# Two v loads of an attention-and-MLP kernel moved on SyncE's queue

## The chip, the cores and the metric

The kernel runs on one core of one Trainium2 chip. The metric is the device time in microseconds (us) of that core, as the median of the runs; smaller is better. Engines are named as in the profile: PE (TensorE, matmul), PEld (its weight loads), DVE (VectorE), ACT (ScalarE), POOL (GpSimd), SP (SyncE, which here only issues DMAs).

## What is computed

Attention over 8 batch rows, 8 heads, 576 positions, head size 64, followed by a two-layer MLP with a squared ReLU. Half of the heads see a sliding window of 32 positions, the other half a dilated one: every fourth position back to 128.

```python
scores = scale * np.matmul(q, k.transpose(0, 1, 3, 2))
mask_plain = (rel >= 0) & (rel < window)                                        # 32
mask_dil = (rel >= 0) & (rel < window * dilation) & (rel % dilation == 0)      # dilation 4
attn = softmax(where(mask, scores, -1e9));  x = attn @ v                        # by head
h = x @ w_in;  out = (np.maximum(h, 0) ** 2) @ w_out                            # 4608 tokens, 512 -> 2048 -> 512
```

## The kernel before

**Rows and stages.** A "row" is one of the 8 batch entries (576 tokens). The MLP works on 9 chunks of 512 tokens. The loop at the end of the kernel (L1039) has one stage for each chunk c from 1 to 8; in stage c the MLP matmuls of chunk c run, and between them, at hand-written steps (`PLANS`, L1023), the parts of the attention of row b = c + 1, and the scores of row b + 1 near the end of the stage. The parts are named by letters (`row_parts`): s0 and s1 are the scores of the sliding heads (PE L638), z0 and z1 those of the dilated ones (PE L653), each followed by the exponential on ACT (L619) and the mask on DVE (L623); a0 to a2 are the products with v of the sliding heads (PE L693), d0, d1, e0, e1 those of the dilated ones (PE L720), each followed by the division on DVE (L676, L677); x and y are transposes of the results on PE (L742, L757), copied by ACT.

**The MLP.** First layer: matmuls at L291, ReLU on ACT (L300), square into `g` on DVE (L325). From stage 2 on the second layer multiplies in seven products of sums (L443), and DVE forms the sums S1 to S3 from `g` (L423 to L429).

**How q, k and v of a row come in.** All tiles here exist once or twice, in turns by the row's parity.

- q and k, sliding heads: POOL asks for `n` (L156); DVE or ACT brings it into token order, `o` (L259 on ACT; for row 4 all of it there; L261 on DVE); SP stores `o` to DRAM, `dp` (`keep_sliding_qk`, L267), and two transposing loads bring it back, `QKTp` (`transpose_sliding`, L275, k first, then q).
- q and k, dilated heads: POOL copies them within DRAM, `dd` (`keep_dilated_qk`, L249); two transposing loads bring them in, `QKTd` (`transpose_dilated`, L279).
- v, dilated heads: two loads of 288 KB into `sd` (`load_dilated_v`, L176 and L180), cast on POOL into `vd` (L235, L237).
- v, sliding heads: six loads of 96 KB into `sv` (`load_sliding_v`, L168), cast on POOL into `vp` (L218, L222). `load_v(b, True)` asks for the dilated loads and then the sliding ones.

**What sets the order.** The schedule is manual: each engine and each queue does its instructions in the order in which the program writes them. All loads of v, the stores, and all transposing loads are on SP's queue; an SP instruction that waits holds all that stand behind it. POOL first does a tiny copy (`see`, L204) that waits for the k half of the last `QKTp`, then asks for `n` and `dd` of the next row, then casts v of the present row.

At the start of stage c (row b = c + 1) the program writes: POOL's look, the loads of `n` and `dd` of row b + 1; from row 4 on SP's `transpose_dilated(b + 1)`; for b = 3 SP's `load_sliding_v(3)`. At step `ORDER[c]` of the stage (46, 33, 9, 2, 2 for c = 1 to 5) it writes `turn_and_load` for row b + 1: the copy into token order, the store, the transposing loads, and the loads of v. Row 3 is turned in stage 1, row 4 in stage 2 (88 to 123 us in the profile), row 5 in stage 3. `CROSS` is 5.

Of the kernel before, what the change touches and what calls it, by code (L numbers as in the profile page):

```python
# [17 lines left out]
def kernel(  # L18
# [134 lines left out]
    def load_whole_sliding_qk(b):  # L153
        n = natp.tile([P, HH, 9, D], FP16, name=f"n{b}", tag="n")
        for i, s in ((1, k), (0, q)):
            nc.gpsimd.dma_start(  # L156
                out=n[64 * i : 64 * (i + 1)],
                in_=s[b, 0:HH].rearrange("h (p j) d -> p h j d", j=9),
            )
        return n  # L160
# [4 lines left out]
    def load_sliding_v(b, m0=0, m1=NB):  # L165
        for m in range(m0, m1):
            lo = QB * m - PADP
            nc.sync.dma_start(  # L168
                out=sv[PADP:P, m, :, :],
                in_=v[b, 0:HH, lo + PADP : lo + P, :].transpose([1, 0, 2]),  # L170
            )

    def load_dilated_v(b, t):
        vv = v[b, HH:H].rearrange("h (i c) d -> i h (c d)", c=DIL)
        if t == 0:
            nc.sync.dma_start(out=sd[PADD:P, 0, :, :], in_=vv[0:QD])  # L176
            return
        if b == 0:
            nc.sync.dma_start(out=sd[0:PADE, 1, :, :], in_=vv[QD - PADE : QD])
        nc.sync.dma_start(out=sd[PADE : PADE + QD, 1, :, :], in_=vv[QD:CL])  # L180

    def load_v(b, dilated_first=False):
        if not dilated_first:
            load_sliding_v(b)
        for t in range(2):
            load_dilated_v(b, t)
        if dilated_first:
            load_sliding_v(b)
# [13 lines left out]
    def see(landed):  # L202

        nc.gpsimd.tensor_copy(look, landed)  # L204
# [34 lines left out]
    def cast_v(b):  # L239
        sliding = [lambda mp=mp: cast_sliding_v(b, mp) for mp in range(NB // 2)]  # L240
        dilated = [lambda t=t, a=a: cast_dilated_v(b, t, a) for t in (0, 1) for a in range(2)]
        return dilated + sliding
# [3 lines left out]
    def keep_dilated_qk(b):  # L246
        d = dpool.tile([2, HH * CL, DIL * D], FP16, name=f"dd{b}", tag="dd")
        for i, src in ((1, k), (0, q)):
            nc.gpsimd.dma_start(  # L249
                out=d[i], in_=src[b, HH:H].rearrange("h (i c) d -> (h i) (c d)", c=DIL)  # L250
            )
        return d

    def in_token_order(b, n):
        o = natp.tile([P, 9, HH, D], FP16, name=f"o{b}", tag="o")
        i = n.rearrange("p h j d -> p j h d")
        j = {2: 6, 3: 6, 4: 9}.get(b, 0)
        if j > 0:
            nc.scalar.copy(o[:, 0:j], i[:, 0:j])  # L259
        if j < 9:  # L260
            nc.vector.tensor_copy(o[:, j:9], i[:, j:9])  # L261
        return o

    def keep_sliding_qk(b, o):
        d = dpool.tile([2, S, HH * D], FP16, name=f"dp{b}", tag="dp")
        for i in (1, 0):
            nc.sync.dma_start(  # L267
                out=d[i].rearrange("(p j) x -> p (j x)", j=9),
                in_=o[64 * i : 64 * (i + 1)].rearrange("p j h d -> p (j h d)"),
            )  # L270
        return d

    def transpose_sliding(b, dp):
        for i in (1, 0):
            nc.sync.dma_start_transpose(out=QKTp[b % 2][:, i, :, PADP:], in_=dp[i])  # L275

    def transpose_dilated(b, dd):
        for i in (1, 0):
            nc.sync.dma_start_transpose(out=QKTd[b % 2][:, i, :, KPAD : KPAD + S], in_=dd[i])  # L279
# [117 lines left out]
    def sum_w_out_gen():  # L397

        for name, pool, tag, w in (("T1", n1p, "nd", 36), ("T2", n1p, "nd", 36), ("T3", n1p, "ns", 36)):
            u = pool.tile([P, w * D], FP16, name=name, tag=tag, bufs=2 if tag == "nd" else 1)  # L400
            T[name] = u[:, 0 : HF * HT].rearrange("p (j t) -> p j t", j=HF)
        for j in range(2):
            f = slice(4 * j, 4 * j + 4)
            b11, b12 = wo[j][:, :, 0:HT], wo[j][:, :, HT:DM]
            b21, b22 = wo[2 + j][:, :, 0:HT], wo[2 + j][:, :, HT:DM]
            for o, a, b in (
                ("T1", b12, b11),
                ("T3", b22, b12),
                ("T2", b22, T["T1"][:, f, :]),
                ("T4", b21, T["T2"][:, f, :]),  # L410
            ):
                nc.vector.tensor_sub(T[o][:, f, :], a, b)
                yield
# [127 lines left out]
    def moe_gen(c):  # L541
        yield from mm1_gen(c)
        yield from mm2_gen(c)

    def moe_seven_gen(c):
        turns["bank"] = 0
        yield from mm1_gen(c, lambda f2: sums_behind(c, f2))
        yield from seven_gen(c)
# [15 lines left out]
    CROSS = 5  # L564
# [231 lines left out]
    def run(*plans, more=()):  # L796


        todo = list(more)
        for plan, parts in plans:  # L800
            for w in plan.split():
                step, *names = w.split(":")
                todo += [(int(step), parts[n]) for n in names]
        at = 0
        for step, part in sorted(todo, key=lambda t: t[0]):
            pump(step - at)
            at = max(at, step)
            part()
        pump(1000)
# [174 lines left out]
    n, dd = load_whole_sliding_qk(2), keep_dilated_qk(2)  # L984
# [2 lines left out]
        for a in range(2):  # L987
            cast_dilated_v(1, t, a)

    def turn(b, n, dd):  # L990
        dp = keep_sliding_qk(b, in_token_order(b, n))
        if b < 4:
            transpose_dilated(b, dd)
        transpose_sliding(b, dp)

    pending.append(mm2_by_rows_gen(0))
    parts = row_parts(1, True)
# [9 lines left out]
            " 25:d1 26:e0 28:e1 29:y0 30:y1",  # L1007
            parts,
        ),
        more=[(25, lambda: turn(2, n, dd))],  # L1010
    )
    load_v(2, True)
    kept[0]()
# [25 lines left out]
    for c in range(1, NTOKC):  # L1039
        b = c + 1  # L1040
        more = []
        casts = cast_v(b) if b < B else []
        if c == 1:

            for cast in casts[:2]:
                cast()
            casts = casts[2:]
            see(sv[PADP : PADP + 1, 3, 0, 0:1])
            more.append((41, kept[1]))
        if b + 1 < B:  # L1050
            see(QKTp[b % 2][0:1, 1, 0, PADP : PADP + 1])
            if b > CROSS:

                see(xT[(b - 1) % RING][0:1, 1, S - 1 : S])
            n, dd = load_whole_sliding_qk(b + 1), keep_dilated_qk(b + 1)

            def turn_and_load(b=b + 1, n=n, dd=dd):
                turn(b, n, dd)
                load_dilated_v(b, 0)
                load_dilated_v(b, 1)  # L1060
                if b > 3 and b <= CROSS:
                    load_sliding_v(b)

            if b + 1 > 3:
                transpose_dilated(b + 1, dd)
            if b == 3:
                load_sliding_v(3)
            more.append((ORDER[c], turn_and_load))
            if b >= CROSS:
                more.append((38, lambda b=b + 1: load_sliding_v(b)))  # L1070
        for cast in casts:
            cast()
        if c == 1:
            it = sum_w_out_gen()
            more += [(2 + 3 * i, lambda it=it: next(it)) for i in range(8)]
        pending.append(moe_gen(c) if c < SEVEN else moe_seven_gen(c))
        now, ahead = PLANS.get(c, ("", ""))
        run((now, rows_.get(b)), (ahead, rows_.get(b + 1)), more=more)
# [30 lines left out]
```

## Time and profile before

| | |
|---|---|
| median of 3 runs | 300.04 us (299.71 to 300.9) |
| the profiled execution's own time | 301.48 us |
| its span, first to last instruction | 299.7 us |
| mean granted TensorE clock | 0.999 |
| PE busy | 287.7 us, 96% of the span |
| DVE, ACT, POOL busy | 202.3, 176.2, 96.6 us |
| DMA moved | 45.59 MB, 152 GB/s over the span |

The profile is one execution, seen instruction by instruction. "Busy" is time in which an engine worked, not in which it was needed: an engine that is idle and is waited for by nobody costs nothing. A line of a timeline gives start, length, engine, line of the kernel, operation, and out<-in tiles; "idle before" and what released the engine follow in brackets. The windows view gives, for each stretch of time, the length, the busy time of PE, PEld, DVE, ACT and POOL with the number of instructions in brackets, the granted clock, the busy share of the DMA engines, and GB/s. The chain of waits is followed back from the last instruction, at each step to what released it.

### The profile page before, as it was taken

To read this page: it belongs to the slowest core of one execution; us is meant where nothing else is said; L and a number is where in the kernel's file an instruction comes from. 1 tells how busy PE (TensorE), PEld (TensorE's weight loads), DVE (VectorE), ACT (ScalarE), POOL (GpSimd) and SP (SyncE) were. 2 spreads that over 40 slices of the span, in tenths; PEclk is the share of its full clock that TensorE was granted. 3 is DMA by queue.
4 is the path that set the end of the run, shared out by engine and by line. 5 is a ranking of instruction groups with operands and counts; after the bars stand their busy time and mean duration, and the time that the engine had idled before them with its cause. 6 is when DMAs were issued, how large, how long until landed. Compare 5 with 4: busy or idle time off the path is not lost.

```text
span 299.7 us, 7125 instructions
## 1 busy us (share of the span) xinstructions
PE 287.7 (96%) x2880; PEld 202.7 (68%) x2880; DVE 202.3 (67%) x371; ACT 176.2 (59%) x331; POOL 96.6 (32%) x153
## 2 busy tenths in 40 slices
PE   2899999999999998999999999999999999999995
PEld 2678945565554577656889988558765875785584
DVE  7686646778633997499688867896878624733662
ACT  1668854778548773766646657664766267425611
POOL 8492009403914604752563019308400000000000
PEclk9999999999999999999999999999999999999999
DMA  7999999799999888998999799989124130003013
GB/s 129 205 159 214 210 212 159 154 174 263 196 195 241 179 154 148 215 270 176 186 229 251 144 169 186 255 187 166 72 92 24 39 131 11 0 2 141 3 35 105
DMA packets 73969, 45.59 MB, mean 152 GB/s; under 512 B 56720, under 2 KB 67600, under 8 KB 73744
## 3 DMA queue, kind: packets, MB, share of 16 engines
q1 hardware_dynamic: 66544, 31.37, 49.0%
q0 software_dynamic: 7248, 13.63, 25.7%
q8 instruction: 22, 0.36, 0.5%
q10 hardware_dynamic: 144, 0.13, 0.1%
q14 instruction: 11, 0.09, 0.1%
HBM read 36.83 MB, written 16.52 MB: 178 GB/s over the span
## 4 chain that ended last, share of the span: by engine, by line
PE 72%; DMA 11%; POOL 6%; DVE 5%; issue 2%; SPq 1%; ACT 1%; POOLq 0%; DVEq 0%; ACTq 0%
PE PS L291 34%; PE PS L443 25%; PE PS L332 6%; DMA nd<-in_k_dram 5%; DMA sv<-in_v_dram 3%; DMA sd<-in_v_dram 3%; PE PS L720 2%; PE PS L693 2%; PE PS L653 1%; POOL vp L222 1%; DVE AT L623 1%; POOL vp L218 1%; ACT AT L619 1%; DVE S L429 1%; PE PS L638 1%
## 5 line engine op out<-in xcount | busy, mean ns | idle before, releaser
L291 PE MATMUL PS<-xr,wi 128*128 128x512 f16 (+3 forms) x704 | 133.5, 341 | 0.3 <-ACT xr L749 0.2
L300 ACT ACTIVATE rt<-PS 128x512 f16<-128x512 f32 (+2 forms) x160 | 88.4, 557 | 42.9 <-PE PS L291 40.0
L291 PEld LDWEIGHTS <-wi 128*128 128x128 f16 x704 | 75.8, 113 | 38.5 <-issue 0.5
L325 DVE TENSOR_TENSOR g<-rt 128x1024 f16<-128x1024 f16 (+1 forms) x64 | 45.7, 714 | 28.6 <-ACT rt L300 28.3
L619 ACT ACTIVATE AT<-PS 128x576 f16<-128x576 f32 x64 | 38.4, 652 | 15.5 <-PE PS L653 8.0
L443 PEld LDWEIGHTS <-S 128*128 128x128 f16 x448 | 42.8, 98 | 6.0 <-issue 0.6
L443 PE MATMUL PS<-T,S 128*128 128x256 f16 x336 | 39.6, 273 | 0.0
L443 PEld LDWEIGHTS <-g 128*128 128x128 f16 x336 | 32.2, 98 | 5.6 <-DVE g L325 0.4
L235 POOL CAST vd<-sd 128x512 f16<-128x512 f32 x32 | 23.6, 762 | 36.8 <-DMA sd<-in_v_dram 36.0
L332 PE MATMUL PS<-wo,g 128*128 128x512 f16 x128 | 33.1, 379 | 0.0
L443 PE MATMUL PS<-wo,g 128*128 128x256 f16 x224 | 26.6, 273 | 0.1
L218 POOL CAST vp<-sv 128x512 f16<-128x512 f32 x24 | 17.2, 716 | 23.3 <-DMA sv<-in_v_dram 16.3
L677 DVE TENSOR_TENSOR y<-PS,rcp 72x512 f16<-72x512 f32 (+1 forms) x32 | 22.0, 687 | 1.1
L623 DVE TENSOR_TENSOR AT<-AT,maskd 128x1152 f16<-128x1152 f16 x14 | 11.5, 818 | 15.2 <-ACT AT L619 15.1
L623 DVE TENSOR_TENSOR AT<-AT,maskp 128x1152 f16<-128x1152 f16 x14 | 14.5, 1036 | 10.3 <-ACT AT L619 10.3
L677 DVE TENSOR_TENSOR x<-PS,rcp 96x512 f16<-96x512 f32 (+1 forms) x25 | 16.6, 665 | 0.9
L222 POOL CAST vp<-sv 32x512 f16<-32x512 f32 (+1 forms) x24 | 16.7, 697 | 1.5
L720 PEld LDWEIGHTS <-AT 128*128 128x128 f16 x256 | 11.9, 100 | 6.8 <-DVE y L677 2.0
L332 PEld LDWEIGHTS <-g 128*128 128x128 f16 x128 | 10.3, 98 | 8.0
L429 DVE TENSOR_TENSOR S<-g,S 128x1024 f16<-128x1024 f16 x14 | 10.7, 804 | 7.4 <-PE PS L443 7.4
L676 DVE RECIPROCAL rcp<-PS 96x8 f32<-96x8 f32 (+3 forms) x57 | 11.2, 197 | 4.9 <-PE PS L720 2.9
L443 PE MATMUL PS<-T,g 128*128 128x256 f16 x112 | 14.2, 273 | 0.0
(93 smaller groups left out, 283.2 us busy)
## 6 DMA issues: line engine op xcount, KB each, us to landing
out_dram<-c SPq DMA_DIRECT2D x12, 512.0 KB
sv<-in_v_dram SPq DMA_DIRECT2D x48, 96.0 KB, 4.9
sd<-in_v_dram SPq DMA_DIRECT2D x16, 288.0 KB
dp<-o SPq DMA_DIRECT2D x12, 288.0 KB
wo<-in_moe_w_out_dram POOLq DMA_DIRECT2D x4, 512.0 KB, 14.3
n<-in_k_dram POOLq DMA_DIRECT2D x6, 288.0 KB, 6.0
n<-in_q_dram POOLq DMA_DIRECT2D x6, 288.0 KB, 6.8
dd<-in_k_dram POOLq DMA_DIRECT2D x6, 288.0 KB, 8.1
```

The lines of the kernel that those rows point to most:

```text
L218: nc.gpsimd.tensor_copy(vp[b % 2][:, m : m + 2, :, 0:D], sv[:, m : m + 2, :, :])
L222: nc.gpsimd.tensor_copy(vp[b % 2][0:PADP, m:m1, :, 0:D], sv[P - PADP : P, m - 1 : m1 - 1])
L235: nc.gpsimd.tensor_copy(o, by_class(sd[:, t]))
L291: nc.tensor.matmul(ph[:, o : o + b - a], w_in_of(dmk, ffc), xr[:, dmk, a:b], start=(dmk == 0 and o == 0), stop=(dmk == NDM - 1 and o + b - ...
L300: nc.scalar.activation(rt, ph[:, 0:w], ACTF.Relu)
L325: nc.vector.tensor_mul(g[:, f2 : f2 + 2, o:TOKC], rt[:, :, o:TOKC], rt[:, :, o:TOKC])
L332: nc.tensor.matmul(po, g[:, ffc, o + t * P : o + (t + 1) * P], w_out_of(ffc), start=(ffc == 0), stop=(ffc == NFF - 1),)
L443: nc.tensor.matmul(po[t], lhs(j)[:, t * P : (t + 1) * P], rhs(j), start=j == 0 and not on_top, stop=j == HF - 1, skip_group_check=on_top,)
L619: nc.scalar.activation(AT[:, u + i, 0:UW], ps[:, :, 0 : UW // 2], ACTF.Exp, scale=scale)
L623: nc.vector.tensor_mul(AT[:, u : u + n, 0:UW], AT[:, u : u + n, 0:UW], mask,)
L677: nc.vector.tensor_tensor(out=x, in0=pv[:, :, :, 0:D], in1=rcp[0:w, 0:i, 0:j].unsqueeze(3).to_broadcast([w, i, j, D]), op=ALU.mult,)
L720: nc.tensor.matmul(pav[:, e, h * (D + 2) : h * (D + 2) + D + 1], AT[:, 4 + 2 * a + t, off : off + P], vd[b % 2][:, t, 2 * a + e, h, 0 : D ...
```

## The change

Three lines are touched in what the program does.

- Stage 2, start: `load_sliding_v(3)`, six issues on SP, stands ahead of `transpose_dilated(4)`, two issues on SP, and no longer behind it.
- Row 4's turn in stage 2: the loads of its v, first the dilated ones and then the sliding ones (eight issues on SP), stand between the store of `o` (`keep_sliding_qk(4)`) and `transpose_sliding(4)`. Before, they stood behind `transpose_sliding(4)`.
- `turn` is written out in `turn_and_load` and keeps its old form for row 2 alone. For rows 2, 3, 5, 6 and 7 the order is as before.

```diff
-    def turn(b, n, dd):
-        dp = keep_sliding_qk(b, in_token_order(b, n))
-        if b < 4:
-            transpose_dilated(b, dd)
-        transpose_sliding(b, dp)
+    def turn(n, dd):
+        dp = keep_sliding_qk(2, in_token_order(2, n))
+        transpose_dilated(2, dd)
+        transpose_sliding(2, dp)
...
             def turn_and_load(b=b + 1, n=n, dd=dd):
-                turn(b, n, dd)
-                load_dilated_v(b, 0)
-                load_dilated_v(b, 1)
-                if b > 3 and b <= CROSS:
+                dp = keep_sliding_qk(b, in_token_order(b, n))
+                if b == 3:
+                    transpose_dilated(b, dd)
+                if b == 4:
+
+                    load_v(b, True)
+                transpose_sliding(b, dp)
+                if b != 4:
+                    load_dilated_v(b, 0)
+                    load_dilated_v(b, 1)
+                if b == CROSS:
                     load_sliding_v(b)
 
+            if b == 3:
+                load_sliding_v(3)
             if b + 1 > 3:
                 transpose_dilated(b + 1, dd)
-            if b == 3:
-                load_sliding_v(3)
             more.append((ORDER[c], turn_and_load))
```

More of the change, by code (lines that the diff above doesn't have):

```diff
@@ L1009 @@
         ),
-        more=[(25, lambda: turn(2, n, dd))],
+        more=[(25, lambda: turn(n, dd))],
     )
```

## The prediction

> **What bounds the kernel now.** I read the page first, then the windows of 2 us around the stretch that the change touches, then the chain of work in order of time, then the timelines of SP, POOL, DVE and PE from 88 to 146 us. TensorE is busy nearly all the time:
>
> ```profile
> PE 287.7 (96%) x2880; PEld 202.7 (68%) x2880; DVE 202.3 (67%) x371; ACT 176.2 (59%) x331; POOL 96.6 (32%) x153
> ```
>
> The other engines end below 70%. So only idle time of PE can be won, and the 12.0 us of it lie mostly at the two ends (6.2 in the first 20 us, 3.5 in the last 20). In the touched stretch the windows give (us, then PE busy, PEld, DVE, ACT, POOL):
>
> ```profile
> 108.00:110.00 2.00, 1.88 (x20) 1.45 (x19) 1.93 (x5) 2.00 (x4) 0.00 (x0) 1.00 1.04 143
> ...
> 112.00:114.00 2.00, 1.48 (x19) 1.13 (x17) 1.97 (x4) 0.00 (x0) 1.87 (x3) 1.00 0.84 182
> ...
> 118.00:120.00 2.00, 1.69 (x21) 1.39 (x18) 1.93 (x6) 0.68 (x3) 0.00 (x0) 1.00 1.22 86
> ...
> 132.00:134.00 2.00, 1.64 (x15) 0.81 (x13) 1.93 (x6) 1.13 (x3) 0.49 (x1) 1.00 1.44 366
> ```
>
> PE lacks 0.12, 0.52, 0.31 and 0.36 us in these four and 0.16 at 134 to 136: 1.47 us in all, 0.5% of the time. That is the whole purse of this change in its own stretch. The 0.52 is the one that it aims at; the chain (start, us, what) shows it:
>
> ```profile
> 106.00 1.29 SPq L279
> 107.39 1.28 SPq L168
> 108.77 0.43 SPq L168
> 109.25 0.46 SPq L168
> 109.82 2.65 DMA sv<-in_v_dram
> 112.54 0.71 POOL vp L222
> 113.29 0.29 PE PS L693 x4
> ```
>
> Row 4's dilated transposes (L279) hold SP until 107.3, only then row 3's sliding v (L168) is asked for, POOL casts it, and PE's first product with it (L693, part a0) starts 0.51 us late. The waits of the windows put those 0.5 us down to POOL vp L222. SP's own order, start and length:
>
> ```profile
> 104.59 2.70 SPq L279 DMA_TRANSPOSE QKTd<-dd  x2
> 107.39 3.89 SPq L168 DMA_DIRECT2D sv<-in_v_dram  x6
> 111.82 1.15 SPq L267 DMA_DIRECT2D dp<-o  x2
> 115.11 2.87 SPq L275 DMA_TRANSPOSE QKTp<-dp  x2
> 118.07 1.36 SPq L176 DMA_DIRECT2D sd<-in_v_dram  x1
> 119.49 0.40 SPq L180 DMA_DIRECT2D sd<-in_v_dram  x1
> 119.99 4.11 SPq L168 DMA_DIRECT2D sv<-in_v_dram  x6
> ```
>
> SP is free at 96.07 (the last store, L362, 95.48 + 0.59) and then stands still for 8.5 us: the waits of SP put it down to dd, which lands at 104.5.
>
> **The change, part by part.** Both edits only move DMA issues on SP; nothing is added or taken away on any engine.
>
> Edit 1: six loads sv (96 KB each) go ahead of two transposes. They come to stand at 96.07, take 3.9 us of SP as now, and are all issued by 100.0, inside the 8.5 us in which SP stood still. Their buffer is free: POOL's casts of row 2 end at 83.3. Landing takes 2.5 us (median now, quiet) to 6.0 us (median of the loads at 120, beside other transfers), so by 102.5 to 106.0. POOL is idle from 102.57 to 111.83 and casts at once.
>
> (a) PE's wait for a0 goes: **-0.51 us**. The next wait, 0.31 at 119.24 (PE L742 for DVE x L677), hangs on part z0's exp and mask, which PE itself starts at 114.82; it moves along and stays.
>
> (b) The six casts take 4.5 us (111.83 to 116.29). They now run at about 104 to 108.5, where DVE is busy 3.86 of 4.00 us, instead of after 111.8. What a cast does to DVE, the lines of g (L325, ns min/median/max) show, first with POOL casting (96.7 to 102.1), then with POOL idle (103.5 to 111.5):
>
> ```profile
> L325 DVE TENSOR_TENSOR g<-rt x3: 1095/1095/1098, 97.3 to 102.0; 128x1024 f16<-128x1024 f16 x3
> L325 DVE TENSOR_TENSOR g<-rt x3: 676/676/678, 103.9 to 108.9; 128x1024 f16<-128x1024 f16 x3
> ```
>
> So +0.42 us for each such operation. Against these very casts the row is milder: two S subtractions (L423) took 1.91 us at 111.88, where 0.68 each is their median: +0.27 each; and g at 159.09 and 188.97 lost nothing beside casts (POOL did). Between 104 and 108.5 stand three: g at 106.15, S at 106.75 and 107.46. Three at 0 to 0.42 is 0 to 1.26; I take three at 0.27, the row of the same casts: **+0.8 us**. It lies on the path: DVE has no gap from 97.3 to 111.0, and PE's weight load waited 0.40 us for g (L325) at 109.64. What DVE wins back at 111.88 (0.54) hides: DVE idles 1.77 us at 116.39 for ACT.
>
> The SBUF — State Buffer page of the Trainium skill ("Who interferes with whom") says that a DVE instruction with two SBUF inputs and a GpSimd one that reads SBUF exclude each other, the second being blocked to the end of the first. The trace agrees in kind: L677, with one input in PSUM, keeps 0.69 us all along. By that rule an operation could wait out a whole cast (0.61), three of them 1.8, and the time would be an estimated 301.3.
>
> (c) Row 4's dilated transposes wait for dd anyway. The added 576 KB share the DMA engines with dd; at the 250 to 280 GB/s of 96 to 102 us that is 0 to 2.3 us, so the pair starts between 104.6 and 106.9 (first one). Its reader, z0 at PE (L653, 114.82), needs it landed, a median of 4.3 us after an issue. The second is issued 1.4 after the first: 108.3 + 4.3 = 112.6 at the latest. Cost **0**, hidden by 2.2 us; if that cover went, PE would wait for the excess.
>
> Edit 2: row 4's eight v loads go between the store of o (dp, L267) and its transposes (L275). Queued behind them on SP: the two transposes, and behind these the stores of the third stage (L483) and row 5's dilated transposes, which wait for dd of row 5 at 130 to 133 in any case. With edit 1, dp no longer waits for SP but for ACT's copy of o (107.39 + 2.10 = 109.49): it goes at 109.6, not 111.82, ended by 110.8. The eight loads take 5.4 us in row 5's turn (143.11 to 148.51), 6.0 in row 4's. So L275 starts at 116.2 to 116.8, not 115.11: **1.1 to 1.7 us later**. Its first transposed half (k) landed just before POOL's look at 120.19, 5.1 us after the issue. 5.1 after 116.2 is 121.3. But 1152 KB of v are now in flight ahead of it on the same queue: at 180 GB/s (112 to 116 us) 6.4 us from about 112.5, to 118.9, where the first transposing packets of before ran 1.1 us after the issue: 1.5 us more. k lands at 121.3 to 122.8, q about 1 us later: 122.3 to 123.8. PE reads it at 124.25 (s0, L638), or 123.7 if (a) came in full. Cost **0**, by a margin of 0 to 2 us. This is the thinnest cover of the change.
>
> POOL's look also holds row 5's loads of n and dd, and row 4's casts. It comes 1.1 to 2.6 us later; n of row 5 then has no v beside it: 5.1 us (row 3, 74 us) or 6.2 (row 7) for its second half instead of 7.8. Issued at 123.1 to 124.0, it lands by 128.2 to 130.2, DVE's copy (L261) stands at 130.78. The casts vd start at 124.3 to 125.8 instead of 123.21 without their waits for sd (0.19 and 0.63); the first is read at 127.71. Cost 0. The casts vp, which now wait until 133.51 with v in hand late, follow at once; they are first read at 136.01, so that gains nothing.
>
> Sum: -0.51 + 0.8 = **+0.3 us**. The profiled execution took 301.48 (span 299.7 and 1.8 around it), 1.4 above the median of the runs; 301.48 becomes 301.8, and the median 300.04 becomes **300.3**.
>
> **The rivals.**
> 1. The casts do no harm. For: at 157 to 160 and 187 to 190 POOL gave way, not DVE. Against: L325's 1.095 in every case from 97 to 102. Then only (a) is left: 300.04 - 0.51 = **299.5**.
> 2. Slower: row 4's sliding transposes land too late for s0. The point is 123.7: if q lands later, PE waits for the excess, and the chain of exp, mask and y behind it (DVE without a gap from 126.1 to 134) shifts by as much, so that nothing is given back. Price: L483 sat 4.5 us on SP at 124.2, right behind the same eight loads; if the transposes are held like that, even half of it (2.25) puts q at 124.5 to 126, up to 2.3 us late: 300.3 + 2 = **302.3**. The DMA: Bandwidth & Descriptors page of the Trainium skill ("Queues, rings and completion order") says that on each DMA engine the descriptors of one ring are consumed in ring order. By that the transposes wait for all of v, which is the 1.5 us above; the trace of before, where nothing of SP's was ahead of them but dp, cannot show it.
> 3. The change does not do what it says: the sv loads are asked for at 96 but land after the stores and beside n and dd, which are still at work at 102, or SP holds them as it held L361 (3.2 us at 92.24); v comes only little before 111, and both terms shrink: **300.0**.
>
> **How the numbers follow.** The forecast (casts cost 0.3 to 1.3, transposes in time) has 0.50, its own range 299.8 to 300.8; rival 1 has 0.20 (299.2 to 299.8); rival 2 has 0.22 (301.0 to 303.5); rival 3 has 0.08. A measurement of this kernel can tell about 0.5% from no change, that is 1.5 us: 298.5 and 301.5. Faster by that needs all 1.47 us of the purse: 0.03. Slower: most of rival 2 (0.18) and the tail of (b) with a late n (0.05): 0.23. The rest, 0.74, is the same. The range 299.4 to 302.2 leaves out half of rival 1 and some two fifths of rival 2.
>
> **What would show it.** In the changed kernel's trace: sv at SP by 96 to 100, and no wait of PE for POOL vp L222 near 113 (edit 1 right); L325 and the S operations between 103 and 111 at 0.9 to 1.1 us instead of 0.68, and PE lacking more than 0.12 us at 108 to 112 (term b right; at 0.68 rival 1 holds); L275 at 116 to 117 and POOL's look at 121 to 123; PE with no gap ahead of L638 near 124 (if there is one, rival 2). The forecast is wrong if sv lands only after 110, or if PE idles over 0.3 us ahead of s0.

## The result and the profile after

| | before | changed |
|---|---|---|
| median of 17 runs | 300.04 us (299.23 to 301.02) | 303.48 us (300.37 to 305.03) |
| ratio, 95% interval | | 1.0080 (1.0059 to 1.0102) |
| the profiled execution, its span | 301.48, 299.7 | 302.32, 300.5 |

The change makes the kernel 0.8% slower, some 2.4 us; the time lies above the predicted range. The ratio is formed from undisturbed runs and is not the quotient of the medians of all runs, which lie 3.4 us apart. The changed kernel's runs fall in two groups by the mean granted clock beside each: nine at 1.000 with a median of 302.1 us, eight at 0.994 with 303.9. The profiled execution is of the first group, near its median. The two spans differ by only 0.8 us because the profiled execution of the kernel before was 1.4 us above that kernel's median.

SP after the change (start, length, line, operation):

```profile
94.62 10.33 SPq L168 DMA_DIRECT2D sv<-in_v_dram  x6
105.11 4.67 SPq L279 DMA_TRANSPOSE QKTd<-dd  x2
110.31 1.14 SPq L267 DMA_DIRECT2D dp<-o  x2
111.55 0.87 SPq L176 DMA_DIRECT2D sd<-in_v_dram  x1
112.47 1.16 SPq L180 DMA_DIRECT2D sd<-in_v_dram  x1
113.73 4.43 SPq L168 DMA_DIRECT2D sv<-in_v_dram  x6
118.27 3.99 SPq L275 DMA_TRANSPOSE QKTp<-dp  x2
122.36 1.73 SPq L483 DMA_DIRECT2D out_dram<-c  x2
```

Row 3's sv is asked for 12.8 us earlier, row 4's transposes (L275) 3.2 us later, and the two stores of stage 2 (L483), which went at 124.20 and took 6.11 us of SP, now go at 122.36 in 1.73. In the kernel before:

```profile
124.20 6.11 SPq L483 DMA_DIRECT2D out_dram<-c  x2
```

There both came behind the requests for row 5's n (120.73 and 121.37): the first held SP for 4.5 us, and the second was issued only at 128.8. Now the first is issued ahead of these requests (123.69 and 124.33), and the second at 123.7, with the first of them. That last move is the one to keep in mind.

The windows of the changed kernel (us, then PE, PEld, DVE, ACT, POOL busy, clock, DMA share, GB/s):

```profile
108.00:110.00 2.00, 1.59 (x16) 1.19 (x14) 1.93 (x5) 2.00 (x4) 1.94 (x2) 1.00 0.52 108
...
112.00:114.00 2.00, 2.00 (x26) 1.82 (x24) 2.00 (x4) 0.45 (x1) 1.33 (x2) 1.00 0.96 237
...
124.00:126.00 2.00, 1.59 (x18) 0.87 (x17) 0.03 (x1) 1.76 (x4) 2.00 (x5) 1.00 1.03 347
...
130.00:132.00 2.00, 1.36 (x13) 0.58 (x12) 1.97 (x4) 1.20 (x2) 1.87 (x3) 1.00 1.39 282
132.00:134.00 2.00, 1.63 (x18) 0.84 (x15) 1.97 (x4) 0.60 (x1) 1.81 (x4) 1.00 0.28 55
```

The 0.52 us at 112 to 114 are won, as wanted; 0.29 more are lost at 108 to 110 (DVE beside POOL's casts). New losses stand at 122 to 126 (0.60: PE's L638 waits for QKTp) and at 130 to 134 (1.01 instead of 0.36). From 120 to 140 us PE is busy 18.25 us instead of 19.48. Of the 1.01 us, 0.64 is a wait for y (L677) that the kernel before does not have, and 0.37 one that it has too (0.36). Where the first comes from, DVE shows, first before, then changed; the last lines are POOL's casts and PE's wait in the changed kernel:

```profile
126.13 0.78 DVE L623 TENSOR_TENSOR AT<-AT,maskp 128x1152 f16<-128x1152 f16 x1 [1.95 <-ACT AT L619]
```

```profile
125.97 1.79 DVE L623 TENSOR_TENSOR AT<-AT,maskp 128x1152 f16<-128x1152 f16 x1 [2.30 <-ACT AT L619]
131.03 0.69 DVE L677 TENSOR_TENSOR y<-PS,rcp 72x512 f16<-72x512 f32 x1
131.64 1.34 DVE L261 COPY o<-n 128x2304 f16<-128x2304 f16 x1
125.94 2.30 POOL L235 CAST vd<-sd 128x512 f16<-128x512 f32 x3
131.77 0.43 PE L720 MATMUL PS<-vd,AT 128*128 128x65 f16 x8 [0.64 <-DVE y L677]
```

The mask (L623) starts as POOL's casts of row 4's vd start, which the late look has moved there, and takes 1.0 us longer. DVE has no gap from there on, so y is late by it.

Row 5's n is no cause of loss in this execution, but it was just in time:

```profile
124.33 6.82 DMA n<-in_q_dram
131.15 0.04 DVEq L261
131.19 0.45 issue
131.64 1.34 DVE o L261
```

DVE's copy of row 5's q and k into token order (L261) needs n and stands between two divisions (y, L677) for which PE waits. It follows the y ahead of it by 0.61 us, as in the kernel before (0.60); an n that lands later than 131.15 would hold it, and the y behind it.

### The profile page after: what moved, and what is told of

It reads as the page before. It is cut to its first block, busy times and chain, and to the rows that moved or that the text cites. A ratio compares the mean times of both kernels' runs of the same rounds, so it can differ in the third digit from the quotient of the medians.

```text
span 300.5 us, 7125 instructions
## 1 busy us (share of the span) xinstructions
PE 287.6 (96%) x2880; PEld 202.1 (67%) x2880; DVE 203.6 (68%) x371; ACT 176.5 (59%) x331; POOL 97.6 (32%) x153
## 4 chain that ended last, share of the span: by engine, by line
PE 64%; DMA 16%; POOL 8%; issue 6%; DVE 4%; ACT 1%; SPq 1%; POOLq 0%; DVEq 0%
PE PS L291 30%; PE PS L443 22%; PE PS L332 6%; DMA sv<-in_v_dram 6%; DMA nd<-in_k_dram 5%; DMA sd<-in_v_dram 3%; DMA n<-in_q_dram 2%; POOL vp L218 2%; PE PS L720 2%; POOL vp L222 2%; PE PS L693 1%; DVE S L429 1%; PE PS L653 1%; ACT AT L619 1%; DVE AT L623 1%
## 5 line engine op out<-in xcount | busy, mean ns | idle before, releaser
L325 DVE TENSOR_TENSOR g<-rt 128x1024 f16<-128x1024 f16 (+1 forms) x64 | 46.7, 730 | 28.1 <-ACT rt L300 27.8
L235 POOL CAST vd<-sd 128x512 f16<-128x512 f32 x32 | 24.6, 794 | 39.0 <-DMA sd<-in_v_dram 38.4
L677 DVE TENSOR_TENSOR y<-PS,rcp 72x512 f16<-72x512 f32 (+1 forms) x32 | 22.0, 686 | 1.1
L623 DVE TENSOR_TENSOR AT<-AT,maskp 128x1152 f16<-128x1152 f16 x14 | 14.3, 1022 | 10.7 <-ACT AT L619 10.7
L623 DVE TENSOR_TENSOR AT<-AT,maskd 128x1152 f16<-128x1152 f16 x14 | 11.6, 829 | 14.3 <-ACT AT L619 14.2
L677 DVE TENSOR_TENSOR x<-PS,rcp 96x512 f16<-96x512 f32 (+1 forms) x25 | 16.6, 665 | 0.9
L222 POOL CAST vp<-sv 32x512 f16<-32x512 f32 (+1 forms) x24 | 15.9, 663 | 1.5
L332 PEld LDWEIGHTS <-g 128*128 128x128 f16 x128 | 10.3, 97 | 8.0
L720 PE MATMUL PS<-vd,AT 128*128 128x65 f16 x256 | 13.7, 197 | 0.8 <-DVE y L677 0.8
```

The lines of the kernel that those rows point to most:

```text
L222: nc.gpsimd.tensor_copy(vp[b % 2][0:PADP, m:m1, :, 0:D], sv[P - PADP : P, m - 1 : m1 - 1])
L235: nc.gpsimd.tensor_copy(o, by_class(sd[:, t]))
L325: nc.vector.tensor_mul(g[:, f2 : f2 + 2, o:TOKC], rt[:, :, o:TOKC], rt[:, :, o:TOKC])
L332: nc.tensor.matmul(po, g[:, ffc, o + t * P : o + (t + 1) * P], w_out_of(ffc), start=(ffc == 0), stop=(ffc == NFF - 1),)
L623: nc.vector.tensor_mul(AT[:, u : u + n, 0:UW], AT[:, u : u + n, 0:UW], mask,)
L677: nc.vector.tensor_tensor(out=x, in0=pv[:, :, :, 0:D], in1=rcp[0:w, 0:i, 0:j].unsqueeze(3).to_broadcast([w, i, j, D]), op=ALU.mult,)
```

## The experiments

Theories: **A**, the loss is the second edit's (A1: row 5's n late, so DVE's copy, y and PE late, and at a long gap the clock; A2: PE's wait for QKTp; A3: POOL's casts beside DVE's masks; later A4: why n is late). **B**, it is the first edit's: the moved casts. **C**, TensorE's clock drops after PE's gaps. Ratios are to the kernel before on the same chip, with 95% intervals.

**The changed kernel again** (`both`, no edit).

> The changed kernel unaltered, for comparison with the parts on one chip. All theories: 301 to 304 us, +2.4 us over before (0.8%). Its times fall in two groups by the mean granted clock that stands beside each: 1.000 (median 302.1 of nine runs so far) and 0.994 (median 303.9 of eight). Theory C (TensorE's clock is halved for a stretch after its gaps near 124 to 134 us) expects runs with 0.994 here too, and, if the profiled one is among them, a stretch of half clock within 10 us behind those gaps.

302.34 us, 1.0063 (1.0034 to 1.0093); 4 of 12 runs at a clock of about 0.994 or below. The profiled one (301.49, look at 122.46) was not among them. In it neither PE waits for QKTp nor DVE for n; the mask takes 1.59 us, and PE waits 0.72 for the y behind it.

**The first edit alone** (`first_only`).

```diff
-                if b == 4:
-                    load_v(b, True)
                 transpose_sliding(b, dp)
+                if b == 4:
+                    load_v(b, True)
```

> Row 3's sv ahead of row 4's dilated transposes; row 4's v stays behind its sliding transposes. Theory A (the loss is the second edit's: late QKTp of row 4, POOL's late look, and what follows): 299.5 to 300.3 us, no wait of PE for QKTp near 124, POOL's look at 119 to 120, clock 1.000 in all runs. Theory B (the loss is the casts of row 3 on DVE's busy stretch): still slower, 301 to 302, with PE idle 0.4 us or more at 108 to 112.

299.96 us beside 300.38, 0.9981 (0.9952 to 1.0009); POOL's look at 117.54. One of 12 runs had a clock of 0.993 (302.43), so "1.000 in all" was not quite met, and the look came before 119. PE lacks 0.42 us at 110 to 112, as B had it, but with the wait for a0 gone the time is not longer. B falls.

**The second edit alone** (`second_only`).

```diff
-            if b == 3:
-                load_sliding_v(3)
             if b + 1 > 3:
                 transpose_dilated(b + 1, dd)
+            if b == 3:
+                load_sliding_v(3)
```

> Row 4's v between the store of o and the transposes; row 3's sv stays behind row 4's dilated transposes. Here v stands ahead of the transposes by as much, and SP reaches the store of o 1.5 us later than in the changed kernel (111.8, not 110.3). Theory A: as slow or slower than both edits, 302 to 305 us, PE waiting 1 to 3 us for QKTp near 124 to 126, POOL's look at 124 to 126. Theory B: about 300.0, no loss without the moved casts.

303.37 us, 1.0075 (1.0049 to 1.0101): A holds, but not as A2 had it. The profiled execution (look at 123.58) has no wait for QKTp. Its DVE idles 1.37 us ahead of L261 "<-DMA n<-in_q_dram", and PE then 1.83 us for y. (It also waits 1.2 us for vp at 113.57, where the kernel before waited 0.51: row 3's v is behind the transposes here.) Behind that gap stands what C looked for; the granted clock is the number ahead of the last two:

```profile
134.00:136.00 2.00, 0.25 (x8) 0.25 (x8) 1.97 (x4) 0.12 (x1) 1.47 (x3) 1.00 0.24 53
136.00:138.00 2.00, 1.84 (x20) 0.88 (x17) 1.90 (x5) 1.20 (x3) 0.00 (x0) 0.82 0.97 188
138.00:140.00 2.00, 2.00 (x6) 0.73 (x5) 1.41 (x3) 0.60 (x1) 0.00 (x0) 0.50 1.06 241
140.00:142.00 2.00, 2.00 (x23) 1.31 (x22) 1.46 (x3) 0.91 (x2) 0.00 (x0) 0.82 0.33 121
```

Only 2 of the 12 runs had a clock of 0.994 or below, and the profiled one is the slowest of all (305.55); the other ten, at 0.999 or 1.000, have a median of 303.3, so most of the loss of this version comes without a lower clock. Half clock for (0.18 + 0.50 + 0.18) x 2 / 0.5 = 3.4 us costs 1.7 us, which is the distance between the two groups of the changed kernel's runs (302.1 and 303.9).

**Only the dilated loads ahead** (`both_dilated`).

```diff
                 if b == 4:
-                    load_v(b, True)
+                    load_dilated_v(b, 0)
+                    load_dilated_v(b, 1)
                 transpose_sliding(b, dp)
+                if b == 4:
+                    load_sliding_v(b)
```

> Both edits, but only the two dilated loads of row 4's v stand ahead of its sliding transposes; the six sliding ones follow behind. SP waits 2.1 us there for the store to land (before: 112.97 to 115.11), and two issues take 0.9, so the transposes lose no time on SP, and 0.6 MB instead of 1.2 MB are ahead of them on the queue. Theory A: QKTp of row 4 lands 1 us later than with the first edit alone or less, no wait of PE near 124, 299.5 to 300.5 us. Theory B: 301 to 302, as with the first edit alone.

300.02 us, 0.9986 (0.9967 to 1.0006), look at 118.73, no clock below 0.998. The six sliding loads ahead of the transposes make the loss.

**POOL's look at v** (`both_look_v`), in stage 3 alone.

```diff
-            see(QKTp[b % 2][0:1, 1, 0, PADP : PADP + 1])
+            if b == 4:
+                see(sv[PADP : PADP + 1, 3, 0, 0:1])
+            else:
+                see(QKTp[b % 2][0:1, 1, 0, PADP : PADP + 1])
```

> Both edits; POOL's look of stage 3 waits for a load of row 4's sv (it lands near 120) instead of for the k half of QKTp (123), so row 5's n and dd are asked for at 120.5 as in the kernel before, not at 123.7, while row 4's transposes stay behind its v. Theory A1 (the late n of row 5 holds DVE's copy L261, and with it y and PE, and at a long gap the clock): most of the loss goes, 300.2 to 301.2 us, no run with a clock of 0.994; the wait for QKTp near 124 stays, 0 to 1 us, perhaps longer since n and dd now run beside the transposes. Theory A2 (the wait of s0 for QKTp is the loss): 302 to 303.5, as with both edits.

302.17 us beside 300.99, 1.0027 (0.9997 to 1.0057): the time lies in A2's range and not in A1's, and the interval overlaps that of `both`, so the times decide nothing. In the profiled execution (300.5 us, look at 119.42) n is in time, as A1 had it, the mask takes 0.84 us, and PE's one long wait is 0.72 us for QKTp. But 5 of 12 runs had a clock of 0.994 or below, two of them at 308.7 and 309.6 us, where A1 expected none. None of these was profiled; that n and dd beside the transposes make QKTp later still in some runs is possible, and was not shown.

**Row 5's n late in the kernel before** (`before_late_loads`).

```diff
+            if b == 4:
+                casts[0]()
+                casts = casts[1:]
             see(QKTp[b % 2][0:1, 1, 0, PADP : PADP + 1])
```

> The kernel before, with the first cast of row 4's v ahead of POOL's look in stage 3: that cast waits for sd (lands at 123.1), so row 5's n and dd are asked for at 123.7 to 124.4 as in the changed kernel, while SP's order and the transposes stay as before. Theory A1: 302 to 304 us, DVE idle ahead of L261 until n lands, PE idle 1 to 2 us behind it, some runs at a clock of 0.994, no wait for QKTp. Theory A2: 300.0 to 300.6.

305.97 us, 1.0154 (1.0119 to 1.0190), the slowest version, above what A1 expected; 5 of 6 runs at 0.994 or below. SP's order is that of before; POOL's remaining casts are later too. The waits from 100 to 140 us, of PE and DVE:

```profile
PE PS L757 <- DVE y L677: 2.6, 1, 2.6
DVE o L261 <- DMA n<-in_q_dram: 2.2, 1, 2.2
```

So row 5's n late, without any change on SP, makes the picture: DVE waits 2.2 us, PE 2.6, and the clock is at 0.61 and 0.53 in the two windows from 136 to 140, which costs another 1.7. PE also waits 0.39 us for the y at 131, behind a mask of 1.23 us beside POOL's casts, and 0.6 more than before for vp near 113. n was asked for late (124.26), behind the stores L483 (from 123.77), and took 8.9 us.

**DVE's copy later** (`both_copy_later`).

```diff
-    ORDER = {1: 46, 2: 33, 3: 9, 4: 2, 5: 2}
+    ORDER = {1: 46, 2: 33, 3: 14, 4: 2, 5: 2}
```

> Both edits; row 5's copy into token order (and with it its store and transposes) at step 14 of stage 3 instead of 9, so that it stands on DVE behind the y of d1 and no longer holds it. Theory A1: 300.5 to 301.3 us, no clock of 0.994, no wait of PE for y over 0.8 us; row 5 has 9 us of slack ahead of its s0, of which this takes 2 to 3. Theory A2: 302 to 303.5, as with both edits.

301.35 us, 1.0019 (0.9996 to 1.0043), all 12 runs at 0.998 or more: about as A1 had it (301.3 at most), but for one wait of PE for y of 1.56 us (limit 0.8). n landed late here too, and the copy then held the next y.

**The casts first** (`both_casts_first`).

```diff
+            if b == 4:
+                for cast in casts[:4]:
+                    cast()
+                casts = casts[4:]
             see(QKTp[b % 2][0:1, 1, 0, PADP : PADP + 1])
```

> Both edits; the six casts of row 4's vd stand ahead of POOL's look in stage 3, so they run at 117.5 to 122, where DVE has two-input operations only at 116.6 to 118 and 121.5, and not at 126 to 131 beside the masks (L623, 1.79 us instead of 0.78 at 125.97) and g. Row 5's n stays at 123.7. Theory A3 (the casts' collision with the masks is a good part of the loss): 301 to 301.7 us, L623 near 126 at 0.78, the wait of PE for y near 131 gone. Theory A1 alone: 302 to 303.5, n still late and its runs with 0.994 still there.

302.64 us, 1.0052 (1.0020 to 1.0083), 3 of 12 runs at 0.994. The time is A1's, but in the profiled execution A3's sign is there as well: the mask at 126.53 takes 1.06 us, and PE's wait for the y near 131 (0.64 in the changed kernel, 0.72 in `both`) is gone. What stands in its place is n, asked for only at 124.69: DVE waits 2.14 us for it, PE 2.60 for the next y. PE's wait near 131 grows with the mask: in the other profiled executions with a late look and a longer mask it is 0.27, 0.39, 0.49, 0.66 and 0.72 us behind masks of 1.11, 1.23, 1.32, 1.50 and 1.59 (`both_stores_later`, `before_late_loads`, `second_only`, `five_stores_later`, `both`). So the casts beside the mask account for the 0.64 and 0.72 us of the changed kernel's two profiled executions; moving them gave no faster kernel here, with n late. Behind this gap of 2.60 us the clock stayed at 1.00, where 1.83 halved it above: the gap's length alone does not decide.

**Five loads ahead** (`both_five`).

```diff
                 if b == 4:
-                    load_v(b, True)
+                    load_dilated_v(b, 0)
+                    load_dilated_v(b, 1)
+                    load_sliding_v(b, 0, 3)
                 transpose_sliding(b, dp)
+                if b == 4:
+                    load_sliding_v(b, 3)
```

> Both edits, but with five of row 4's eight v loads ahead of its sliding transposes and three behind, between the two dilated ones alone (300.0 us, POOL's look at 118.7) and all eight (302.3, look at 122.5 to 123.2). If the loss grows with the lateness of the look (theory A1): look at 120 to 121.5, 300.3 to 301.5 us, a clock of 0.994 in at most one run in six. A rival, that the loss comes from any sliding v ahead of the transposes, whatever the time: 302 or more.

302.26 us beside 301.03, 1.0036 (1.0012 to 1.0060), 2 of 12 runs at 0.994; the look came at 120.69, nearly as before, and still DVE waited 2.15 us for n and PE 2.60 for y, again at full clock. The time is the rival's. So A1 needed mending: it is not the late look alone that makes n late. In every version in which n was late the two stores L483 were issued from 121.1 to 123.8, ahead of the request for n's second half, by 0.5 to 1.8 us. Versions with n in time have the stores near there too (before, `both_dilated` and `both_look_v`: from 121.7 to 124.2), but behind that request, by 1.1 to 2.8 us. The changed kernel and `both` have them ahead by 2.0 and 1.8, with n just in time.

**The stores held back** (`both_stores_later`, `five_stores_later`): the two stores of stage 2 behind row 5's dilated transposes on SP.

```diff
+            def put():
                 nc.sync.dma_start(out=out[t0 : t0 + HT, w].rearrange("(t p) m -> p t m", p=P), in_=o)
+            held.append(put) if c == 2 else put()
...
+        if c == 3:
+            more += [(6, lambda put=put: put()) for put in held]
```

> Both edits, with the two 512 KB stores of stage 2 put behind row 5's dilated transposes on SP (they wait for dd of row 5). Theory A4 (the stores, which edit 2 lets go 2 to 5 us earlier, share the DMA engines with row 5's n and make it late): the second half of n lands 5 to 6 us after its issue, not 7 to 9, DVE's copy L261 does not wait for it, PE idles less than 0.8 us at a time behind it, no clock of 0.994; 300.5 to 301.3 us, 0.6 us of it the wait for QKTp near 124 that stays. If the late look alone is to blame: n still lands 7 us or more after its issue, 302 to 303.

> The version with five v loads ahead of the transposes, with the same two stores held back. Theory A4: n lands before 128.5, no wait of L261, no clock of 0.994, 300.0 to 300.6 us. If any sliding v ahead of the transposes costs the time in another way: 301.7 to 302.5, as without.

301.34 us beside 300.62, 1.0022 (0.9993 to 1.0051), and 300.70, 1.0000 (0.9972 to 1.0028), each 0.1 us or less above A4's range; all 24 runs at 0.998 or more, where 6 of 24 were lower without this edit, and no wait of L261, nor the one of PE for QKTp that A4 had left in. The second half of n from issue to landing (us, last number), first with five loads ahead, then the same with the stores held back:

```profile
n<-in_q_dram POOLq DMA_DIRECT2D x1, 288.0 KB, 9.5
```

```profile
n<-in_q_dram POOLq DMA_DIRECT2D x1, 288.0 KB, 5.1
```

With both edits it goes from 6.8 (changed kernel) or 7.3 (`both`) to 4.9. In `five_stores_later` the look came even later (122.23, n's second half issued at 123.4, not 122.0), n landed by 128.5, and the time was that of before. The DMA queues show how. In the changed kernel POOL's queue, which carries n, moved nothing from 123.7 to 127, the first 3.3 us after the request, while SP's moved 1.00 MB, as much as the two stores have; in `both_stores_later` it began about 1.4 us after the request (122.04), and SP's queue moved nothing from 123 to 127. A4 holds for n and for the clock: the stores ahead of n make it late. On time alone the gain is less sure, since each interval overlaps that of the version without the edit. The masks beside POOL's casts stay (1.11 and 1.50 us, PE waits 0.27 and 0.66 for y behind them): the held stores do nothing for A3.

**In search of a better version**: the copy at step 14 (the edit of `both_copy_later`) on the kernel before, on the first edit, and on the version with the dilated loads ahead.

> The kernel before with only row 5's copy into token order at step 14 of stage 3 instead of 9. If the copy's place is worth something by itself, 299.5 to 299.8 us (PE idle at 132 to 136 was 0.5); if not, 300.0 to 300.5, the same as before.

> The first edit alone with row 5's copy at step 14 of stage 3. The first edit alone took 299.96 beside 300.38 for the kernel before (0.9952 to 1.0009). If that small gain is real and the copy's place adds to it: 299.4 to 299.8, an interval wholly below 1; if neither is: 300.2 to 300.6.

> Both edits with only the dilated loads of row 4's v ahead of its transposes, and row 5's copy into token order at step 14 of stage 3. If DVE's copy between two divisions by the row sums is what keeps PE waiting for y (0.5 us at 132 to 134 in the version with the dilated loads alone), that wait shrinks and the time is 299.3 to 299.8, 0.3 to 0.4% below the kernel before; if the wait only moves to the next y (as 1.56 us did with both edits), 300.0 to 300.3.

300.90 us, 0.9994 (0.9976 to 1.0011): the copy's place alone is worth nothing. 299.86, **0.9962 (0.9947 to 0.9976)**: the first edit with the later copy beats the kernel before by 0.4%, beside 301.03. 300.18, 0.9973 (0.9953 to 0.9994), with a wait of 0.56 us for y left. In the profiled execution of the best one PE's waits from 104 to 140 us are 0.42 for g and 0.20 for x, and of the 0.52 us that PE lacked at 132 to 136, 0.15 is left: the two edits together remove both waits, the first that for v, the later copy that for y.

## Why the prediction was wrong

**The bound and the purse** were right: PE decides, and nothing above 0.5% was to be won. The best version found wins 0.38%.

**(a), the wait for a0, -0.51**: right. PE's L693 follows at 112.66 without a wait. The way there was wrong in size: SP took 10.3 us for the six issues beside the stores, n and dd, not 3.9, and POOL cast from 107.0, not 104.

**(b), the casts beside DVE, +0.8**: right on DVE, too dear on PE. Three S operations went from 0.69 to 0.98 us, 0.9 in all; two of the changed kernel's:

```profile
109.72 0.98 DVE L425 TENSOR_TENSOR S<-g 128x1024 f16<-128x1024 f16 x1
110.74 0.98 DVE L427 TENSOR_TENSOR S<-S,g 128x1024 f16<-128x1024 f16 x1
```

Each lost 0.29 us, near the 0.27 taken from the same casts. PE lost 0.29 at 108 to 110 and 0.07 at 110 to 112, since only what stood ahead of g at 109.0 held it. The prediction's other price, a whole cast for each operation by the SBUF — State Buffer page of the Trainium skill ("Who interferes with whom"), was 1.8 on DVE; the measured 0.9 is half of it. So the first edit alone is -0.51 + 0.36, about -0.15, and with the 0.20 that PE now waits at L653 about zero; measured 0.9981 with an interval that holds 1.

**(c), the dilated transposes**: right, no wait for them.

**Edit 2, L275 at 116.2 to 116.8, look at 121.3 to 122.8, cost 0**: measured 118.27 and 123.15; the v issues took 6.6 us of SP, and the store ahead of them went 0.7 later. Rival 2's mechanism came, at 0.60 us instead of 2: the thin cover was named, its use was not put into the sum. It is not in every execution (none in `both`). The 1.5 us added for v ahead of the transposes does not show behind the issue: the k half landed 4.9 us after L275 began, 5.1 in the kernel before; the delay stood in SP's issues.

**The step that failed** is the paragraph on POOL's look, which puts both things that the look delays at "Cost 0".

The first is "n of row 5 then has no v beside it ... it lands by 128.2 to 130.2". It took v away from beside n and did not ask what comes in its place. The stores L483 had been named as queued behind the transposes, but not priced: with v gone from behind the transposes they are issued by 123.7, ahead of n's second half, 1 MB on the same DMA engines. n took 6.8 us in the changed kernel, and up to 9.5 in its variants, instead of the 5.1 or 6.2 of the sum; it was asked for at 124.33 instead of by 124.0, and landed at 131.15, with nothing left of the cover. Where it lands later still, DVE's copy holds y and PE: `before_late_loads` shows that a late n is enough for a loss of this kind, `both_stores_later` and `five_stores_later` that without the stores beside it n is in time even after a late look, and the runs with a lower clock are gone.

The second is the casts vd, "Cost 0" because the first is read late enough. What they do to DVE meanwhile was priced for row 3's casts in (b), and not for these: the mask took 1.79 us instead of 0.78 beside them, and PE lost 0.64.

**The clock** was in no part of the prediction: behind a gap of PE of 1.8 to 2.6 us it was halved for 3.4 us in two of the four profiled executions with such a gap, at a price of 1.7 us. The changed kernel's nine runs at full clock have a median of 302.1, just inside the predicted range; the eight others, at 303.9, put the median outside. Among 122 runs of the kernel before beside the experiments none had a clock below 0.998. What of the 0.8% is wait and what clock can be read from the groups only roughly: 302.1 against 300.0 for the first, 1.7 us in 8 of 17 runs for the second.

**Left open**: how the loss of the changed kernel itself is shared out. Its two profiled executions, both at full clock, show the wait for QKTp (0.60 and none) and the mask beside the casts (0.64 and 0.72), and n just in time; none of its runs with the lower clock was profiled, and that n was late in them is argued from the variants. Open as well: why the clock fell behind 1.83 us and not behind 2.60, and what happened in the five runs of `both_look_v` with a low clock.

## What to carry to other kernels

When a load is moved forward on a queue, price what moves up into its old place as well: here two stores that nobody had touched ran into the next row's load. A delayed engine brings its work to another place, so price what it meets there too: here casts that ran into a mask. Look for what an in-order engine does between two results that PE waits for; a copy there turns a late load into a gap of PE. A gap near 2 us costs more than itself where the clock can drop.

## What the runs showed of the hardware that was not expected

- The granted clock fell to 0.50 for 3.4 us behind PE gaps of 1.83 us (`second_only`) and 2.62 us (`before_late_loads`), and not behind gaps of 2.60 us (`both_casts_first` and `both_five`). The Trainium skill (TensorE: Matmul & The Clock Gate, "Part 1: The HAM clock gate") has half clock after about 3.4 us of idleness in a free-running window. The half and the 3.4 us agree with these traces; the idleness does not, since gaps well under 3.4 us were enough twice.
- Six issues of 96 KB loads took SP 10.3 us in one place (changed kernel, 94.62) and 3.9 in another (before, 107.39). The mean busy share of the DMA engines meanwhile was the same, 1.06 and 1.08, and does not tell the two apart.
- DVE's copy L261 took 1.34 us beside POOL's casts (157.00, 186.87) and without them (130.78), all in the kernel before, while operations with two inputs in SBUF went from 0.69 to 0.98 (L427, changed kernel) and the mask from 0.78 to 1.79 (L623).
